# Three token groups' h1 transposed by DMA instead of TensorE, and 28 more blocks of the MLP's first product computed during attention

## The chip, the cores and the metric

One core of a Trainium2 chip runs the whole program. The metric is device time in microseconds (us); lower is better. The engines are TensorE (PE; PEld is its weight loading), VectorE (DVE), ScalarE (ACT), GpSimd (POOL), and SyncE (SP), whose queue issues every DMA of this kernel in program order.

## The reference

All tensors are bf16. S = 2048 tokens, D = 512, F = 1792, 32 heads of 16 columns.

```python
mod = (silu(c) @ w_mod).reshape(1, 6, 1, 512)
sa, ca, ga, sb, cb, gb = mod[:, 0], ..., mod[:, 5]
h = layernorm(x) * (1 + ca) + sa
q, k, v = split_heads(h @ wqkv)                 # 32 heads of 16
p = softmax(where(0 <= i - j < 256, q @ k.T / 4, -1e9))
x = x + ga * (merge_heads(p @ v) @ wo)
h = layernorm(x) * (1 + cb) + sb
h = layernorm(h)                                # the mixer's own norm
u = gelu(einsum('bsd,sf->bdf', h, w1) + b1)     # B1: product over the tokens
y = einsum('bdf,fs->bds', u, w2) + b2           # B2
out = x + gb * y.transpose(0, 2, 1)
```

## The kernel before

**Stages.** A start-up stage loads the inputs, makes the modulation columns `modFM` and the first token group's `h1T`. Attention follows, then a tail with what is left of B1, then B2 with the output.

**Attention.** The 2048 tokens are four groups `tg` of 512 (four row tiles `tl` of 128). In each group the 32 heads are four sets `g8` of 8. Each set has five *units* (k = 0 to 4); so a group is 20 units, numbered `ul` = 5 * g8 + k, and all of attention is 80. A unit is two score tiles `pss` (each two PSUM banks; three buffers), two exponentials `et` on ScalarE (L584), and the products with V into `po`, which has one PSUM bank. After units k = 2 and k = 4 VectorE transposes `po` out of PSUM (`t`, L643); GpSimd divides (`merge`), VectorE transposes back (`OTd`). In group 0 the units k = 0 and k = 3 have half-sized exponentials.

**Dense groups.** The other TensorE work of attention is laid by hand on units in `plan(tg)`: at most one *dense group* a unit. A dense group is 16 column-tiled matmuls (L279, `dense`) into the single PSUM buffer `dn`, which VectorE must empty before the next group may start. There are groups for V (`v_group`), Q and K (`qk_group`), the output projection (`wo_group`, followed by a chain `ln23` of two norms that gives `hb`), and B1 partial sums (`part_group`). In the program, the first exponential of unit u comes first, then the scores of unit u+1, the dense group of unit u, its evacuation, and the products of unit u-1.

**h1T.** For `tg` = 1 to 3, GpSimd applies the first norm (`apply_by_pool`, tile `xn1`, four buffers); TensorE transposes it in two groups of eight 128x128 transposes through `dn` (L261, units 10 and 11 in group 0, 11 and 12 in groups 1 and 2); VectorE evacuates and modulates it in one instruction (L269, `h1T`, one buffer).

**B1 partial sums.** B1 is 14 column blocks `fc` by 16 token blocks `sc`. For the four `fc` in `PART`, `sc` = 0 to 7 are summed in group 3 (32 blocks; two dense groups each, L279 with `hb` and `w1a`) and copied to SBUF (`part`, L742). The tail does the rest: `fc` 0 to 5 for all `sc` (L951), then `fc` 6 to 13 in pairs (L1037), where a partial sum is added back on VectorE (`gelu_a`, L960) before the gelu on ScalarE (L962).

**Order of the engines' work.** It is written out by hand (`manual_schedule`). A planner with estimated clocks (`clock`) decides only where the VectorE chains (norm statistics, norm applications, `norm_rest`, `ln23`) are put between the fixed steps: `fill(until)` places a step if its cost fits. `at_unit` issues the loads: `paced` lets one load follow the first exponential of a unit. On SP's queue the copies of V into `Vc` (L621), the `wmod`, `wod` and `w1a` loads (L793), the `bc` broadcast (L343, L345) and then the `w1b` and `w2r` loads (L933, L935) follow each other in program order. `w1a` holds the first NA token blocks of w1 and is loaded during attention; `w1b` holds the others and is loaded, like `w2r`, into the space that attention frees.

Of the kernel before, what the change touches and what calls it, by code (L numbers as in the profile page):

```python
# [24 lines left out]
NA = 10  # L25
# [5 lines left out]
def kernel(  # L31
# [61 lines left out]
    opool = ctx.enter_context(tc.tile_pool(name="opool", bufs=2))  # L93

    PART = (6, 7, 8, 9)
# [81 lines left out]
    qpool = tc.alloc_tile_pool(name="qpool", bufs=2)  # L177
# [3 lines left out]
    hpool = tc.alloc_tile_pool(name="hpool", bufs=1)  # L181
# [59 lines left out]
    def ln1_apply(tg, tl):  # L241
        xn1[tg, tl] = xp.tile([P, D], DT.bfloat16, name="xn1")
        mean, rstd = ln1[tg][:, tl, 0:1], ln1[tg, tl // 2][:, tl % 2 : tl % 2 + 1]
        if tg:
            apply_by_pool(xn1[tg, tl][:], xres[4 * tg + tl][:], mean, rstd)
        else:
            nc.vector.tensor_scalar(
                out=xn1[tg, tl][:], in0=xres[4 * tg + tl][:], scalar1=mean, scalar2=rstd,
                op0=ALU.subtract, op1=ALU.mult,
            )  # L250


    def transpose_group(tg, pair, pool):
        def mms():
            if pair == 0:
                h1T[tg] = hpool.tile([P, ND, 4 * P], DT.bfloat16, name="h1T")
            pt = pool.tile([P, 2, 4 * P], DT.bfloat16, name="dn")
            for n in range(2):
                dc = 2 * pair + n
                for tl in range(4):  # L260
                    nc.tensor.transpose(  # L261
                        pt[:, n, tl * P : (tl + 1) * P], xn1[tg, tl][:, dc * P : (dc + 1) * P], identity[:]
                    )
            return pt

        def evac(pt):
            for n in range(2):
                dc = 2 * pair + n
                nc.vector.tensor_scalar(  # L269
                    out=h1T[tg][:, dc, :], in0=pt[:, n, :], scalar1=modFM[:, 4 + dc : 5 + dc],  # L270
                    scalar2=modFM[:, dc : dc + 1], op0=ALU.mult, op1=ALU.add,
                )
        return mms, evac, 1.2
# [10 lines left out]
    def v_group(tg, tl, pool, name="dn"):  # L284
        def mms():
            pv = pool.tile([P, D], DT.float32, name=name)
            for dc in range(ND):
                dense(
                    pv, lhsT=h1T[tg][:, dc, tl * P : (tl + 1) * P],
                    rhs=wqkv[:, dc, 2 * D : 3 * D], start=(dc == 0), stop=(dc == ND - 1),  # L290
                )
            return pv

        def evac(pv):
            nc.vector.tensor_copy(out=VaugT[tg][:, tl, :, 0:DH], in_=pv[:].rearrange("p (h d) -> p h d", d=DH))  # L295
            if tl > 1:
                nc.vector.tensor_copy(out=Vc[0][0:64, tl, 0:8, :], in_=VaugT[tg][0:64, tl, 0:8, :])
        return mms, evac, 0.9 if tl > 1 else 0.7

    def qk_group(tg, g8, kind, pool):  # L300
        col0 = g8 * P + (D if kind == "k" else 0)

        def mms():
            pq = pool.tile([P, 4 * P], DT.float32, name="dn")
# [7 lines left out]
        def evac(pq):  # L312
# [5 lines left out]
            QT[tg][g8] = qpool.tile([P, 2, 4 * P], DT.bfloat16, name=f"QT{g8}")  # L318
# [77 lines left out]
    with tc.manual_schedule():  # L396

        with tc.tile_pool(name="modps", bufs=1, space=bass.MemoryType.PSUM) as modps, tc.tile_pool(
# [98 lines left out]
            QT[0][0] = qpool.tile([P, 2, 4 * P], DT.bfloat16, name="QT0")  # L497
# [150 lines left out]
        def norm_rest(tg, g8):  # L648
# [12 lines left out]
            def back():  # L661
                OTd[tg][g8] = opool.tile([P, 4 * P], DT.bfloat16, name=f"OTd{g8}")
                nc.vector.transpose(out=OTd[tg][g8][:], in_=m[:])
# [36 lines left out]
        live = set()  # L700
        loaded = set(range(8))
# [26 lines left out]
        def part_group(fc, k):  # L728
            def mms():
                assert done >= set(range(4 * k, 4 * k + 4))  # L730
                if k == 0:
                    part[fc, "ps"] = ps_dn.tile([P, D], DT.float32, name="dn")
                for sc in range(4 * k, 4 * k + 4):
                    dense(
                        part[fc, "ps"], lhsT=w1box["a"][:, sc, fc * P : (fc + 1) * P], rhs=hb[sc][:],
                        start=(sc == 0), stop=(sc == 7),
# [3 lines left out]
            def evac(ps):  # L740
                if k == 1:
                    nc.vector.tensor_copy(out=part[fc][:], in_=ps[:])  # L742
            return mms, evac, 0.7 * k
# [4 lines left out]
        def plan(tg):  # L748
# [17 lines left out]
            else:  # L766
                for ul, g8, kind in ((2, 1, "k"), (3, 2, "q"), (4, 2, "k"), (5, 3, "q"), (8, 3, "k")):
                    qk(ul, tg, g8, kind)
                for ul in (6, 7, 9, 10):
# [3 lines left out]
            if tg + 1 < NG:  # L773
                t0, t1, q0, v0, k0, q1, v1 = (10, 11, 12, 16, 14, 15, 18) if tg == 0 else (11, 12, 13, 14, 15, 17, 18)
                lay(t0, transpose_group(tg + 1, 0, ps_dn))
                lay(t1, transpose_group(tg + 1, 1, ps_dn))
                lay(v0, v_group(tg + 1, 0, ps_dn))
                lay(v1, v_group(tg + 1, 1, ps_dn))
                for ul, g8, kind in ((q0, 0, "q"), (k0, 0, "k"), (q1, 1, "q")):
                    qk(ul, tg + 1, g8, kind)  # L780
            else:
                for n, fc in enumerate(PART):
                    for k in range(2):
                        lay(12 + 2 * n + k, part_group(fc, k))
# [11 lines left out]
        def at_unit(tg, ul, u, behind):  # L796
            if ul == 0 and tg + 1 < NG:
# [4 lines left out]
                def ap(tl):  # L802
                    ln1_apply(tg + 1, tl)
                    return 1.13
                add_chain((st(1) if tg == 0 else []) + [(lambda tl=tl: ap(tl), 0.0) for tl in range(4)], first=True)
# [62 lines left out]
        for u, (tg, g8, k) in enumerate(units):  # L868
            ul = 5 * g8 + k
            if ul == 0:  # L870
# [149 lines left out]
    with tc.tile_pool(name="gtmp", bufs=2) as gtmp:  # L1020
# [9 lines left out]
        for n, fg in enumerate(fgroups[2:]):  # L1030
            pu = ps_u[n % 2].tile([P, 2, D], DT.float32, name=f"pu{n % 2}")
            for sc in range(NT):
                for i, fc in enumerate(fg):
                    s0 = 8 if fc in PART else 0
# [75 lines left out]
```

## Time and profile before

| What | Value |
|---|---|
| median of 3 runs | 266.26 us (265.99 to 266.61) |
| profiled execution: its own time, and its span in the trace | 268.42 us, 266.7 us |
| mean granted TensorE clock | 0.986 |
| busy share of the span: PE, PEld, DVE, ACT, POOL | 91%, 49%, 63%, 61%, 49% |
| exponentials (L584) | 160, busy 143.6 us |
| start-up, until the first exponential | 17.5 us |
| attention, first to last exponential | 17.5 to 168.9 us |
| rest of B1: L951, then L1037 | to 194.1 us, then to 214.8 us |
| B2 (L1073) | 214.8 to 263.2 us |

How to read it: times are counted from the start of the span. The profiled execution took 1.7 us more than its span, and 2.2 us more than the median of the runs. Shares are averages over stages with different limits: ScalarE is the fullest engine during attention and does little afterwards. In the chain of waits a step is followed back to what released it. In a timeline row the columns are start, duration, engine, line, operation, and the idle time before it with its releaser.

### The profile page before, as it was taken

The numbers are of one execution on the slowest core, as the hardware profiler recorded it, in microseconds if no ns is written. First come the engines' busy times: TensorE is split into PE (matmuls) and PEld (weight loads), VectorE is DVE, ScalarE is ACT, GpSimd is POOL, SyncE is SP. The second block draws the span as 40 slices with busy tenths as digits, with TensorE's granted clock in tenths as the row PEclk, the third lists the DMA queues.
The fourth block names the chain that finished last, engine by engine and source line by source line (L and its number), as shares of the span: only waits on it lengthen the run. The fifth ranks groups of instructions, "written<-read, shape, count | busy, mean of one in ns | idle before, by whom it ended". The sixth has DMA issues, their size and how long they took to land.

```text
span 266.7 us, 11081 instructions
## 1 busy us (share of the span) xinstructions
PE 243.6 (91%) x4933; PEld 129.7 (49%) x4933; DVE 166.9 (63%) x348; ACT 163.7 (61%) x189; POOL 129.4 (49%) x222
## 2 busy tenths in 40 slices
PE   6878988979899889988898999999999999999994
PEld 2434554545555455554555555544444444444443
DVE  6449777886688788798696787689511000523454
ACT  6748887999999999999999999300091110000000
POOL 6102773769476899988997298965200000000000
PEclk9799979999999999999999999999999999999999
DMA  5906984215644534000022000899900000202031
GB/s 173 360 21 160 261 238 153 84 47 144 206 143 112 138 108 117 4 5 5 12 74 72 5 2 5 286 416 420 387 11 0 2 1 0 79 2 79 13 106 39
DMA packets 26084, 29.95 MB, mean 112 GB/s; under 512 B 3252, under 2 KB 23476, under 8 KB 26036
## 3 DMA queue, kind: packets, MB, share of 16 engines
q1 hardware_dynamic: 26036, 29.25, 34.5%
q8 instruction: 38, 0.62, 1.0%
q14 instruction: 10, 0.08, 0.1%
HBM read 22.55 MB, written 2.23 MB: 93 GB/s over the span
## 4 chain that ended last, share of the span: by engine, by line
PE 70%; DVE 18%; ACT 5%; issue 3%; DMA 2%; SPq 1%; ACTq 0%; DVEq 0%
PE py L1073 18%; PE dn L279 18%; PE pu L1037 8%; PE pu L951 7%; PE pss L534 5%; ACT et L584 5%; PE po L595 4%; DVE t L643 3%; PE po L611 3%; DVE qs L317 2%; DVE VaugT L295 2%; DMA wmod<-in_w_mod_dram 2%; PE pss L541 2%; DVE KT L314 2%; DVE x L378 1%
## 5 line engine op out<-in xcount | busy, mean ns | idle before, releaser
L584 ACT ACTIVATE et<-pss 128x1024 bf16<-128x1024 f32 (+1 forms) x160 | 143.6, 992 | 10.0 <-PE pss L541 7.2
L1073 PE MATMUL py<-guT,w2r 128*128 128x512 bf16 (+1 forms) x238 | 48.5, 366 | 0.0
L1052 DVE SCALAR_TENSOR_TENSOR o<-py,bFM,bc 128x512 bf16<-128x512 f32 (+1 forms) x17 | 11.7, 715 | 44.4 <-PE py L1073 44.4
L279 PE MATMUL dn<-h1T,wqkv 128*32 128x512 bf16 x512 | 34.0, 387 | 4.0 <-DVE qs L317 1.5
L534 PE MATMUL pss<-QT,KT 32*128 32x64 bf16 (+2 forms) x704 | 29.6, 237 | 7.6 <-ACT et L584 4.7
L1073 PEld LDWEIGHTS <-w2r 128*128 128x128 bf16 x238 | 23.3, 98 | 25.3
L643 DVE STREAM_TRANSPOSE t<-po 128x512 f32<-128x512 f32 x32 | 22.8, 711 | 12.2 <-PE po L611 11.9
L215 POOL TENSOR_SCALAR ln_ve<-ln_mv 128x1 f32<-128x1 f32 (+1 forms) x40 | 9.5, 237 | 37.2 <-DVE ln_mv L237 20.4
L534 PEld LDWEIGHTS <-KT 32*128 32x128 bf16 x704 | 15.7, 92 | 23.8 <-issue 14.0
L219 POOL TENSOR_TENSOR ln_rstd<-ln_ve,mhalf 128x1 f32<-128x1 f32 (+1 forms) x40 | 23.9, 599 | 3.3
L595 PE MATMUL po<-et,VaugT 128*32 128x64 bf16 (+2 forms) x704 | 25.0, 241 | 0.0
L595 PEld LDWEIGHTS <-VaugT 128*32 128x32 bf16 x704 | 17.2, 96 | 10.8 <-issue 1.7
L279 PEld LDWEIGHTS <-wqkv 128*32 128x32 bf16 x512 | 13.0, 97 | 14.3 <-issue 7.2
L655 POOL TENSOR_TENSOR merge<-t,zr 128x512 bf16<-128x512 f32 x16 | 17.0, 1061 | 5.3 <-DVE zr L654 5.3
L541 PE MATMUL pss<-mask_q,mask_k 32*128 32x256 bf16 (+1 forms) x256 | 19.4, 261 | 0.0
L279 PE MATMUL dn<-wqkv,h1T 128*32 128x512 bf16 x240 | 15.7, 380 | 1.3 <-DVE qs L317 0.8
L962 ACT ACT_TABLE_LOAD x1 | 1.3, 1283 | 24.9 <-PE pu L951 24.9
L687 POOL TENSOR_TENSOR h<-h,bc 128x512 bf16<-128x512 bf16 x12 | 14.0, 1169 | 3.9 <-DVE h L683 3.9
L279 PE MATMUL dn<-wod,OTd 128*32 128x512 bf16 x192 | 12.6, 381 | 2.1 <-DVE KT L314 1.0
L688 POOL TENSOR_TENSOR h<-h,bc 128x512 bf16<-128x512 bf16 x12 | 13.9, 1156 | 0.9
L951 PE MATMUL pu<-hb,w1a 128*128 128x512 bf16 x60 | 13.5, 379 | 0.0
L611 PE MATMUL po<-et,Vc 128*32 128x64 bf16 x960 | 13.0, 194 | 0.0
(110 smaller groups left out, 363.4 us busy)
## 6 DMA issues: line engine op xcount, KB each, us to landing
w2r<-in_B_w_dram SPq DMA_DIRECT2D x14, 512.0 KB, 10.6
w1a<-in_B_w_dram SPq DMA_DIRECT2D x20, 224.0 KB, 2.9
w1b<-in_B_w_dram SPq DMA_DIRECT2D x6, 448.0 KB, 6.3
Vc<-VaugT SPq DMA_DIRECT2D x32, 64.0 KB, 2.5
wmod<-in_w_mod_dram SPq DMA_DIRECT2D x8, 256.0 KB, 4.3
out_dram<-otile SPq DMA_DIRECT2D x15, 128.0 KB, 1.7
x<-in_A_x_dram SPq DMA_DIRECT2D x6, 256.0 KB, 4.5
Vc<-VaugT SPq DMA_DIRECT2D x12, 128.0 KB, 3.6
```

Source lines behind the costliest of these rows:

```text
L219: nc.gpsimd.tensor_tensor(out=r[:], in0=ve[:], in1=mhalf[:, 0:n], op=ALU.pow)
L279: nc.tensor.matmul(out[cols, :], lhsT=lhsT[:, cols], rhs=rhs, start=start, stop=stop, tile_position=(0, 32 * j), skip_group_check=True,)
L534: nc.tensor.matmul(pss[j // 2][:, j % 2, c0 : c0 + nq], lhsT=keys(kb, g8)[rows[j], k0 : k0 + P], rhs=QT[tg][g8][rows[j], par, q0 : q0 + nq ...
L541: nc.tensor.matmul(pss[j // 2][:, j % 2, :].rearrange("p (a r) -> p a r", a=2)[:, 0:n, :] .rearrange("p a (b q) -> p a b q", q=64)[:, :, 0 ...
L584: act = nc.scalar.activation(out=et[:, :, 0:n], in_=state.pop((u, a))[:, :, 0:n], func=ACT.Exp, scale=SCORE_SCALE,)
L595: nc.tensor.matmul(state["po"][32 * j : 32 * j + 32, q0 : q0 + nq], lhsT=VaugT[kb // 4][:, kb % 4, 8 * g8 + 2 * j + par, :], rhs=state["e" ...
L611: nc.tensor.matmul(state["po"][32 * j : 32 * j + 32, q0 : q0 + 64], lhsT=Vc[half][:, b, 8 * g8 + 2 * j + par, :], rhs=state["e", tg, g8, 2 ...
L643: nc.vector.transpose(out=state["t2"][:, par, :], in_=state["po"][:])
L655: nc.gpsimd.tensor_tensor(out=m[:].rearrange("p (b a d) -> p a b d", a=2, d=DH), in0=t2v[:, :, :, 0:DH], in1=zr[:].to_broadcast([P, 2, 16, ...
L951: nc.tensor.matmul(pu[:, i, :], lhsT=w1_of(sc, fc), rhs=hb[sc][:], start=(sc == 0), stop=(sc == NT - 1),)
L1037: nc.tensor.matmul(pu[:, i, :], lhsT=w1_of(sc, fc), rhs=hb[sc][:], start=(sc == s0), stop=(sc == NT - 1),)
L1073: nc.tensor.matmul(pys[n][:, 0 : hi - lo], lhsT=w2r[:, fc, tb * P : (tb + 1) * P], rhs=guT[fc][:, lo:hi], start=(fc == 0), stop=(fc == NF ...
```

## The change

- The transposes of `h1` for groups 1 to 3 leave TensorE. `turn` issues, for each row tile, one DMA transpose of a 128x512 tile from SBUF to SBUF (12 in all, on SP's queue); `modulate` then multiplies and adds in SBUF in place (12 instructions on VectorE, each over one 128x512 slice that needs all four transposes of its group). The planner holds a `modulate` back until four units after the last transpose was issued by its clocks. `h1T` gets two buffers.
- The first norm is applied by VectorE for groups 2 and 3; GpSimd keeps group 1.
- The dense groups are laid anew. Units without one: in group 0 units 9 to 12 and 14 (before 9, 17, 19); in group 1 units 11 and 12 (before 16 and 19); in groups 2 and 3 none (before 16 and 19, and 11).
- `PART` covers fc 6 to 12 for sc 0 to 7 and fc 13 for sc 0 to 3: 60 blocks instead of 32. fc 10, 11 and 12 are summed in two parts, with an added VectorE sum (`part += dn`). The tail's pairs then do 68 matmuls instead of 96.
- NA is 8 instead of 10: `w1a` is 16 loads instead of 20, `w1b` 8 instead of 6.
- The QT tiles share one pool of six buffers; `OTd` 2 and 3 have one buffer each.

```diff
-NA = 10
+NA = 8
...
-    PART = (6, 7, 8, 9)
+    PART = {6: 8, 7: 8, 8: 8, 9: 8, 10: 8, 11: 8, 12: 8, 13: 4}
...
-    hpool = tc.alloc_tile_pool(name="hpool", bufs=1)
+    hpool = tc.alloc_tile_pool(name="hpool", bufs=2)
...
     def ln1_apply(tg, tl):
...
-        if tg:
+        if tg == 1:
             apply_by_pool(xn1[tg, tl][:], xres[4 * tg + tl][:], mean, rstd)
         else:
             nc.vector.tensor_scalar(
...
-    def transpose_group(tg, pair, pool):
...
+    def turn(tg, tl):
+        if tl == 0:
+            h1T[tg] = hpool.tile([P, ND, 4 * P], DT.bfloat16, name="h1T")
+        dma.dma_start_transpose(out=h1T[tg][:, :, tl * P : (tl + 1) * P], in_=xn1[tg, tl][:])
+
+    def modulate(tg, dc):
+        nc.vector.tensor_scalar(
+            out=h1T[tg][:, dc, :], in0=h1T[tg][:, dc, :], scalar1=modFM[:, 4 + dc : 5 + dc],
+            scalar2=modFM[:, dc : dc + 1], op0=ALU.mult, op1=ALU.add,
+        )
...
-        def part_group(fc, k):
+        def part_group(fc, ks, k):
...
             def evac(ps):
-                if k == 1:
+                if k != ks[-1]:
+                    return
+                if ks[0]:
+                    nc.vector.tensor_tensor(out=part[fc][:], in0=ps[:], in1=part[fc][:], op=ALU.add)
+                else:
                     nc.vector.tensor_copy(out=part[fc][:], in_=ps[:])
...
-                for ul, g8, kind in ((2, 1, "k"), (3, 2, "q"), (4, 2, "k"), (5, 3, "q"), (8, 3, "k")):
+                for ul, g8, kind in (
+                    ((2, 1, "k"), (3, 2, "q"), (4, 2, "k"), (5, 3, "q"), (8, 3, "k")),
+                    ((2, 2, "k"), (3, 3, "q"), (4, 3, "k")),
+                    ((2, 3, "q"), (3, 3, "k")),
+                )[tg - 1]:
...
-                for ul in (6, 7, 9, 10):
+                for ul in (6, 7, 9, 10) if tg == 1 else (5, 6, 7, 9):
...
+            for ul, what, n in (
+                ((15, "q", 0), (16, "k", 0), (17, "v", 0), (18, "v", 1), (19, "q", 1)),
+                ((13, "q", 0), (14, "v", 0), (15, "k", 0), (16, "k", 1), (17, "q", 1), (18, "v", 1), (19, "q", 2)),
+                ((12, "q", 0), (13, "v", 0), (14, "k", 0), (15, "k", 1), (16, "q", 1), (17, "v", 1), (18, "q", 2),
+                 (19, "k", 2)),
+                (),
+            )[tg]:
...
+            places, parts = {
+                2: ((8, 10, 11), ((10, (0,)), (11, (0,)), (12, (0,)))),
+                3: (
+                    (4, 8, 10, 11, *range(12, 20)),
+                    ((13, (0,)), (10, (1,)), (11, (1,)), (12, (1,)), *((f, (0, 1)) for f in (6, 7, 8, 9))),
+                ),
+            }.get(tg, ((), ()))
...
                 def ap(tl):
                     ln1_apply(tg + 1, tl)
-                    return 1.13
-                add_chain((st(1) if tg == 0 else []) + [(lambda tl=tl: ap(tl), 0.0) for tl in range(4)], first=True)
+                    turn(tg + 1, tl)
+                    turned[tg + 1] = 20 * tg + now[0] + 4
+                    if tg == 0:
+                        on_pool(1.13)
+                add_chain((st(1) if tg == 0 else []) + [(lambda tl=tl: ap(tl), 0.42 * (tg > 0)) for tl in range(4)]
+                          + [(lambda dc=dc: modulate(tg + 1, dc), 0.42, lambda: 20 * tg + now[0] >= turned[tg + 1])
+                             for dc in range(ND)], first=True)
...
-                    s0 = 8 if fc in PART else 0
+                    s0 = PART.get(fc, 0)
```

## The prediction

> **What bounds the kernel now.** I read the chain of waits first, for the tail, then timelines of ScalarE, TensorE and VectorE, for attention. End of the chain (start, us, what):
>
> ```profile
> 172.99 1.25 PE pa L973 x5
> ...
> 177.26 16.84 PE pu L951 x78
> 194.10 20.72 PE pu L1037 x96
> 214.81 48.40 PE py L1073 x238
> ```
>
> After attention TensorE works without a gap, so a matmul taken out there shortens the run by its own length. ScalarE in attention:
>
> ```profile
> 39.31 2.92 ACT L584 ACTIVATE et<-pss 128x1024 bf16<-128x1024 f32 x4 [0.55 <-PE pss L571]
> 43.58 2.92 ACT L584 ACTIVATE et<-pss 128x1024 bf16<-128x1024 f32 x4 [1.35 <-PE po L611]
> 46.91 1.94 ACT L584 ACTIVATE et<-pss 128x1024 bf16<-128x1024 f32 x2 [0.42 <-PE pss L541]
> ...
> 100.33 35.88 ACT L584 ACTIVATE et<-pss 128x1024 bf16<-128x1024 f32 x38 [0.62 <-PE pss L541]
> 136.37 9.66 ACT L584 ACTIVATE et<-pss 128x1024 bf16<-128x1024 f32 x10 [0.16 <-PE pss L541]
> ```
>
> From group 1 on ScalarE sets the pace: 38 exponentials in 35.88 us, 0.944 each, 1.89 us a unit. Its waits after 39 us in group 0 are 0.55 + 1.35 + 0.42 = 2.3 us, around the two transpose groups. TensorE where each unit already has a dense group (units 13 to 18 of group 3):
>
> ```profile
> 157.43 1.05 PE L279 MATMUL dn<-hb,w1a 128*32 128x512 bf16 x16
> ...
> 163.33 1.05 PE L279 MATMUL dn<-hb,w1a 128*32 128x512 bf16 x16 [0.24 <-DVE part L742]
> ...
> 166.89 1.91 PE L279 MATMUL dn<-hb,w1a 128*32 128x512 bf16 x32
> ```
>
> Five units take 166.89 - 157.43 = 9.46 us, and ten exponentials 9.44: with every unit filled the two engines are level, with nothing to spare.
>
> **The change part by part.**
>
> *B1 out of the tail.* 96 matmuls take 20.72 us, 0.216 each; 28 fewer: **-6.0 us**. The four added `gelu_a` sums and the gelus ride beside them: a pair still takes 16 x 0.216 = 3.45 us, longer than its two sums (2 x 0.69, by L960) or its two gelus (2 x 0.73); the last pair's end about 0.69 + 0.69 + 0.73 = 2.1 us into B2, which needs them only after 48 matmuls, 10 us. Without that cover they would cost 2.1. Two more `w1b` loads (448 KB each, 0.92 MB at about 410 GB/s, 2.2 us): `w2r`'s last issue is at 185.1 and lands 8 to 11 us later, so near 198 after; B2 then starts near 209. Zero.
>
> *Entering the tail.* One statistics step (0.64 + 0.18 us) instead of two lies ahead of the last `OTd`; GpSimd's `merge` (1.06) then limits: **-0.4**.
>
> *Dense work in attention.* Seven more dense groups, +7 x 1.05 = 7.4 us of TensorE; six transpose groups go, of 0.61 to 1.03 each, about -4.4. ScalarE hides it while it is the slower: groups 2 and 3 now have 40 filled units, 8 stretches of five. At 9.46 against 9.44 this is +0.2; if the 0.24 us wait for `dn` falls due on half of the units, +4.8. VectorE decides which. In group 2 it was busy 32.6 of 38.7 us; it gains four norm applications and four modulations (8 x 0.54, by L683's mean), three `part` copies and one more evacuation (4 x 0.68) and loses four L269 (0.535 each): 4.3 + 2.7 - 2.1 = +4.9, less what of the `ln23` chains slips into group 3, so about 90% instead of 84%. As 38 exponentials ran without a wait at 84%, I take **+1.0**. GpSimd loses 8 x (0.27 + 0.77) = 8.3 us; it ends nothing there.
>
> *Thin stretches.* Group 1 now has two empty units running, group 0 four. The trace shows a price for that (busy us of PE, PEld, DVE, ACT, POOL, then granted clock, DMA share, GB/s):
>
> ```profile
> 34.00:37.00 3.00, 1.85 (x49) 1.09 (x49) 2.41 (x7) 2.93 (x5) 2.79 (x6) 1.00 0.73 198
> 37.00:41.00 4.00, 4.00 (x104) 2.56 (x92) 2.54 (x6) 3.45 (x4) 2.43 (x4) 0.57 0.89 283
> ```
>
> Three us with TensorE busy 62% were followed by about 3.5 us at half clock. Units 11 and 12 of group 1 will be as thin for 4.6 us, just ahead of filled ones; 3.5 us at half clock lose 1.75 us of TensorE work. Between 0 and 1.75 I take **+0.8**. (The Trainium skill, "TensorE: Matmul & The Clock Gate", section "What's actually happening", says that the clock halves after an idle window of about 3.4 us. Read strictly, 62% busy is no idle window and this term would be 0, the total 0.8 lower; the rows above speak for the harsher reading.)
>
> *The DMA transposes.* The trace has none. The nearest rows are the copies between SBUF tiles, in the table of DMA issues (KB each, us to landing) and in SP's timeline:
>
> ```profile
> Vc<-VaugT SPq DMA_DIRECT2D x32, 64.0 KB, 2.5
> Vc<-VaugT SPq DMA_DIRECT2D x12, 128.0 KB, 3.6
> ```
>
> ```profile
> 30.90 1.25 SPq L621 DMA_DIRECT2D Vc<-VaugT  x2
> 32.83 1.25 SPq L621 DMA_DIRECT2D Vc<-VaugT  x2
> 34.18 3.24 SPq L793 DMA_DIRECT2D wmod<-in_w_mod_dram  x5
> ```
>
> An SBUF-to-SBUF copy of 128 KB lands after 3.6 us, and copies follow each other after 0.63. So four transposes are done between 3 x 0.63 + 2.5 = 4.4 us after the first issue (overlapping) and 4 x 3.6 = 14.4 (one by one); a gain is excluded, since nothing used these DMAs before. I take the lower end with 3.6 to land, as the copies overlap. A `modulate` waits in VectorE's order, and evacuations queue behind it. In group 1, by the order of the changed program, the fourth transpose is issued near 61.2 and `modulate` follows unit 5's Q copy at 67.3; in group 2, 100.1 and 106.1. Six us cover 3.6: no cost. Group 0 is tighter. GpSimd starts the four applications at 30.60 and needs 1.1 us each, so the fourth transpose is issued near 35.0, but `modulate` stands right behind this row:
>
> ```profile
> 34.74 0.15 DVE L357 CAST bFM<-dn 128x30 f32<-128x30 bf16 x1
> ```
>
> It stalls from 34.9 to 38.6, and the next `po` evacuation (37.41 before), with three modulations and an `OTd` ahead of it, comes near 40.9. ScalarE has then up to three score buffers in hand, 2.8 us, so some 0.7 of the 3.5 shows. On SP's queue the transposes stand ahead of two `Vc` copies and the five `wmod` loads: the last of these is issued near 39.4 instead of 36.8, lands 4.3 later near 43.7, and the `bc` product wants it near 41.5 (43.3 before, less the transposes). TensorE waits 2, of which some 1 reaches ScalarE. Against this stand the 2.3 us of waits around the removed transposes. Group 0 between -2.3 and +4: I take **-0.5**.
>
> Sum: -6.0 - 0.4 + 1.0 + 0.8 - 0.5 = **-5.1 us**. On the profiled execution's 268.42 us that is 263.3; on the median of the runs, which lies 2.16 below, 266.26 - 5.1 = **261.1 us**.
>
> **The rivals.**
>
> *Slow transposes (slower).* One mechanism: the four transposes of a group run one by one, t us each, and `modulate` stalls VectorE, with `dn` and `po` unemptied behind it. With the first issue at 31.7, 58.7 and 97.3, `modulate` at 34.9, 67.3 and 106.1, and 2.8 us of scores in hand, groups 0, 1 and 2 lose 4t - 6.0, 4t - 11.4 and 4t - 11.6. At t = 2.8 the first loss (5.2) eats the whole gain; at 3.6, the landing of a like copy, the loss is 8.4 + 3.0 + 2.8 = 14.2 and the time 275. For it: no row shows a transpose, and each element of a row goes to another partition. Against it: copies of the same size overlap. Chance 0.30. (The Trainium skill, "VectorE: DVE Perf Modes", section "The three transpose paths", gives 1309 ns for a 128x128 block by DMA; if the four blocks of a tile add up, an estimate from it is t = 5.2 and a time of 295. No run here shows it.)
>
> *VectorE or `dn` binds in the filled groups.* The +4.8 end: 265. Against it: the 38 exponentials without a wait at 84%. Chance 0.13.
>
> *Attention gains too.* Group 0 gets its whole 2.3, no thin stretch costs anything, filled units run level: -6.0 - 0.4 - 2.3 + 0.2 = -8.5, or 257.8. Chance 0.11.
>
> **How the numbers follow.** The forecast, 259 to 264, has 0.46. Faster by over 0.2% (0.5 us, about what a measurement of this kernel can tell from none): all of the forecast, 0.11, 0.09 of the second rival, 0.02 of the first (t under 2.7): 0.68. Within 0.2%: 0.02 + 0.02. Slower: 0.26 of the first and 0.02 of the second. The range reaches from the third rival to t = 3.3 of the first: 257.5 to 272.
>
> **What would show it.** Right: L1037's successor takes 68 matmuls and 14.7 us; attention ends within 2 us of its old end; transposes land within 4 us; no VectorE idle ahead of `modulate` outside group 0. Wrong: idle time ahead of `modulate` released by a DMA in groups 1 and 2; `dn` waits on most units of groups 2 and 3; a clock under 1 after unit 12 of group 1 for more than 3.5 us.

## The result, and the profile after

The changed kernel takes **272.92 us** (median of 4 runs, 272.71 to 274.01) against 266.12 beside it: ratio **1.025, 95% interval 1.0202 to 1.0298**, so it is slower by 5.4 to 7.9 us. Ratios here and below leave disturbed runs out, so they can differ a little from the ratio of two medians; of e2 that leaves two runs of four, and e2's profile is of a disturbed one. The forecast was 261.1, faster.

The profiled execution has a span of 272.3 us (266.7 before) and a mean TensorE clock of 0.962 (0.986). I divide both spans at the same events: a group of attention is 40 exponentials and reaches from the start of its first to the start of the next group's first.

| stretch, us | before | after | difference |
|---|---|---|---|
| start to first exponential | 17.5 | 15.5 | -2.0 |
| group 0 | 36.2 | 43.8 | +7.7 |
| group 1 | 38.2 | 42.8 | +4.6 |
| group 2 | 38.7 | 39.2 | +0.6 |
| group 3 | 38.4 | 39.0 | +0.6 |
| last exponential to B2 | 45.9 | 40.0 | -5.9 |
| B2 to the end | 51.9 | 51.9 | 0.0 |

The first row differs between executions of one kernel too (15.4 to 17.9 over the profiles of this study), so it is no effect of the change. The other rows are the change's: the tail gave what was promised, and two groups of attention lost twice as much (12.3 against 5.9 us). Differences are taken before rounding.

The end of the chain of waits (start, us, what) answers to the lines of L951, L1037 and L1073 before. The product that took 96 matmuls and 20.72 us now takes 68 and 14.63:

```profile
205.71 8.42 PE pu L1058 x39
214.18 6.21 PE pu L1058 x28
220.38 4.53 PE py L1094 x21
```

ScalarE in attention (start, us; the bracket is the idle time before, and who ended it). Groups 2 and 3 look as before, batches of 18 and 20 exponentials without a wait. Groups 0 and 1 do not:

```profile
42.81 1.08 ACT L579 ACTIVATE et<-pss 128x512 bf16<-128x512 f32 x2 [4.22 <-PE pss L536]
48.61 1.08 ACT L579 ACTIVATE et<-pss 128x512 bf16<-128x512 f32 x2 [2.20 <-PE pss L536]
53.70 2.92 ACT L579 ACTIVATE et<-pss 128x1024 bf16<-128x1024 f32 x4 [1.78 <-PE pss L566]
71.00 4.82 ACT L579 ACTIVATE et<-pss 128x1024 bf16<-128x1024 f32 x5 [4.00 <-PE pss L536]
...
110.83 17.21 ACT L579 ACTIVATE et<-pss 128x1024 bf16<-128x1024 f32 x18 [0.93 <-PE pss L536]
128.21 18.96 ACT L579 ACTIVATE et<-pss 128x1024 bf16<-128x1024 f32 x20 [0.17 <-PE pss L536]
```

**Group 0** is read on three queues. SP's queue (how long each issue held it), then VectorE, then TensorE:

```profile
31.03 7.18 SPq L258 DMA_TRANSPOSE h1T<-xn  x4
38.26 1.27 SPq L616 DMA_DIRECT2D Vc<-VaugT  x2
39.63 2.60 SPq L808 DMA_DIRECT2D wmod<-in_w_mod_dram  x5
```

```profile
32.73 0.15 DVE L352 CAST bFM<-dn 128x30 f32<-128x30 bf16 x1
39.55 0.41 DVE L261 TENSOR_SCALAR h1T<-h1T,modFM 128x512 bf16<-128x512 bf16 x1 [6.66 <-DMA h1T<-xn]
```

```profile
41.88 0.40 PE L590 MATMUL po<-et,VaugT 128*32 128x256 bf16 x4 [5.35 <-DVE t L638]
45.65 1.04 PE L328 MATMUL dn<-wmod,sT_rep 128*32 128x512 bf16 x8 [0.50 <-DMA wmod<-in_w_mod_dram]
```

The four transposes hold SP's queue for 7.18 us. VectorE stands 6.66 us behind its first modulation, with the evacuation of `po` queued behind; TensorE waits 5.35 us for that evacuation and ScalarE 4.22 for TensorE's scores. Then the product for `bc` still waits for `wmod`, 0.9 us in all. The issue of `wmod`'s last load ends at 42.2, which is 26.8 us after the first exponential; before it was 37.4, or 19.9 us after.

The queue had no room for them. Some lines of SP's timeline of the kernel before:

```profile
23.58 3.35 SPq L793 DMA_DIRECT2D x<-in_A_x_dram  x2
...
27.61 2.08 SPq L621 DMA_DIRECT2D Vc<-VaugT  x2
...
37.52 0.93 SPq L793 DMA_DIRECT2D wod<-in_A_wo_dram  x2
```

From 19.20 to 38.45 its rows add up to 18.3 of 19.25 us: what is put into a full queue delays everything behind it by nearly its whole length, here by 26.8 - 19.9 = 6.9 of 7.18 us.

TensorE's clock in the same stretch (us; busy us of PE, PEld, DVE, ACT, POOL; granted clock, DMA share, GB/s):

```profile
32.00:35.00 3.00, 1.79 (x49) 1.01 (x49) 0.79 (x2) 2.92 (x5) 2.90 (x5) 1.00 0.96 171
35.00:38.00 3.00, 1.51 (x76) 0.91 (x65) 0.00 (x0) 3.00 (x4) 1.31 (x3) 0.82 0.71 50
38.00:41.00 3.00, 0.00 (x0) 0.00 (x0) 1.46 (x4) 0.59 (x1) 0.00 (x0) 0.50 0.50 117
...
54.00:57.00 3.00, 2.58 (x64) 1.34 (x59) 1.73 (x4) 2.62 (x4) 0.87 (x2) 1.00 0.00 0
```

The half clock begins at 36.9 us: a mean of 0.82 from 35 to 38 is 1.1 us at 0.50. That is only 0.4 us after TensorE's last matmul (36.5), and in the 3.4 us before it TensorE was busy for 2.49. So the long wait did not bring the drop about. The kernel before has one at nearly the same place (37.3 us, after 2.26 busy of 3.4), and so has e1 below, which does not have the waits; there it lasts 3.4 us. Here, with the waits behind it, it lasts 17 us, until 54.0.

**Group 1** is another story. VectorE's norms for group 2, and GpSimd's foldings of `wod` beside them, from the two timelines:

```profile
63.66 3.51 DVE L249 TENSOR_SCALAR xn<-x,ln_mv,ln_rstd 128x512 bf16<-128x512 bf16 x3
...
68.19 0.40 DVE L249 TENSOR_SCALAR xn<-x,ln_mv,ln_rstd 128x512 bf16<-128x512 bf16 x1
```

```profile
64.68 3.51 POOL L804 TENSOR_TENSOR wod<-wod,bc 128x512 bf16<-128x512 bf16 x3
```

Three norms take 1.17 us each while GpSimd's operations of 1.17 run; the fourth, alone, takes 0.40. The copy of V behind the three comes late, TensorE waits 2.85 us for it, and ScalarE the 4.00 us at 71.00.

### The profile page after: what moved, and what is told of

Same layout as the page of the kernel before. It is cut to its first block, busy times and chain, and to the rows that moved or that the text cites. A ratio compares the mean times of both kernels' runs of the same rounds, so it can differ in the third digit from the quotient of the medians.

```text
span 272.3 us, 11163 instructions
## 1 busy us (share of the span) xinstructions
PE 240.4 (88%) x4960; PEld 128.6 (47%) x4969; DVE 178.0 (65%) x367; ACT 164.7 (60%) x189; POOL 121.7 (45%) x206
## 3 DMA queue, kind: packets, MB, share of 16 engines
HBM read 22.55 MB, written 2.23 MB: 91 GB/s over the span
## 4 chain that ended last, share of the span: by engine, by line
PE 63%; DVE 22%; DMA 4%; POOL 4%; SPq 3%; issue 2%; ACT 1%; DVEq 0%; ACTq 0%; POOLq 0%
PE dn L272 20%; PE py L1094 18%; PE pu L972 8%; PE pu L1058 5%; DMA wmod<-in_w_mod_dram 4%; DVE VaugT L289 3%; PE pss L529 3%; DVE t L638 3%; DVE KT L309 3%; PE po L590 3%; PE po L606 2%; DVE qs L312 2%; DVE xn L249 2%; DVE ln_stats L666 2%; PE pa L994 1%
## 5 line engine op out<-in xcount | busy, mean ns | idle before, releaser
L272 PE MATMUL dn<-h1T,wqkv 128*32 128x512 bf16 x512 | 35.1, 397 | 8.0 <-DVE VaugT L289 5.8
L529 PE MATMUL pss<-QT,KT 32*128 32x192 bf16 (+2 forms) x704 | 27.9, 243 | 4.8 <-ACT et L579 2.3
L1073 DVE SCALAR_TENSOR_TENSOR o<-py,bFM,bc 128x512 bf16<-128x512 f32 (+1 forms) x17 | 11.7, 716 | 30.5 <-PE py L1094 30.5
L590 PE MATMUL po<-et,VaugT 128*32 128x64 bf16 (+2 forms) x704 | 25.8, 247 | 5.4 <-DVE t L638 5.4
L590 PEld LDWEIGHTS <-VaugT 128*32 128x32 bf16 x704 | 18.6, 98 | 17.0 <-issue 7.5
L529 PEld LDWEIGHTS <-KT 32*128 32x128 bf16 x704 | 14.7, 93 | 20.1 <-issue 11.7
L272 PE MATMUL dn<-hb,w1a 128*32 128x512 bf16 x240 | 15.5, 380 | 1.7 <-DVE part L743 1.2
L272 PE MATMUL dn<-wod,OTd 128*32 128x512 bf16 x192 | 12.6, 381 | 2.9 <-DVE x L373 1.3
L682 POOL TENSOR_TENSOR h<-h,bc 128x512 bf16<-128x512 bf16 x12 | 13.9, 1155 | 2.0 <-DVE h L678 2.0
L981 DVE TENSOR_TENSOR gelu_a<-pu,part 128x512 f32<-128x512 f32 x8 | 5.2, 686 | 14.6 <-PE pu L1058 14.6
L316 POOL TENSOR_SCALAR QT<-qs,mask_even 128x512 bf16<-128x512 bf16 x14 | 9.8, 703 | 10.8 <-DVE qs L312 10.8
```

The costliest lines, as they stand in the source:

```text
L272: nc.tensor.matmul(out[cols, :], lhsT=lhsT[:, cols], rhs=rhs, start=start, stop=stop, tile_position=(0, 32 * j), skip_group_check=True,)
L529: nc.tensor.matmul(pss[j // 2][:, j % 2, c0 : c0 + nq], lhsT=keys(kb, g8)[rows[j], k0 : k0 + P], rhs=QT[tg][g8][rows[j], par, q0 : q0 + nq ...
L590: nc.tensor.matmul(state["po"][32 * j : 32 * j + 32, q0 : q0 + nq], lhsT=VaugT[kb // 4][:, kb % 4, 8 * g8 + 2 * j + par, :], rhs=state["e" ...
L682: nc.gpsimd.tensor_tensor(out=h2[:], in0=h2[:], in1=bc_cb1, op=ALU.mult)
```

## The experiments

Two theories for the loss. **Queue theory:** the transposes lengthen SP's full queue, so that `wmod` and the modulations are late (group 0), and the foldings collide with VectorE's new norms (group 1). **Rivals:** that the place of the modulations alone is at fault, that TensorE's half clock in the emptied units is the cause, or that transposes of this kind are slow wherever they stand. Each edit is one of the changed kernel, unless it names another. "Against before" is the ratio less one, times 266.3 us.

| run | edit | median | ratio (95%) | against before, us |
|---|---|---|---|---|
| after | | 272.9 | 1.0250 (1.0202 to 1.0298) | +6.7 |
| e1 | group 1's h1 on TensorE | 263.7 | 0.9902 (0.9865 to 0.9939) | -2.6 |
| e2 | foldings later | 272.4 | 1.0130 (1.0051 to 1.0209) | +3.5 |
| e3 | e1 and e2 | 264.0 | 0.9890 (0.9825 to 0.9955) | -2.9 |
| e4 | modulations later | 273.7 | 1.0266 (1.0202 to 1.0329) | +7.1 |
| e5 | transposes behind `wmod` | 268.6 | 1.0041 (0.9995 to 1.0087) | +1.1 |
| e6 | `wmod` loaded earlier | 271.6 | 1.0149 (1.0090 to 1.0209) | +4.0 |
| e7 | e1 without the 28 blocks | 268.5 | 1.0047 (1.0003 to 1.0092) | +1.3 |
| e8 | matmuls in the empty units | 273.4 | 1.0213 (1.0145 to 1.0280) | +5.7 |
| e9 | e5 and e2 | 266.5 | 0.9965 (0.9916 to 1.0014) | -0.9 |
| e10 | e9, earlier loads and transposes | 271.6 | 1.0179 (1.0102 to 1.0255) | +4.8 |
| e11 | e1, foldings earlier | 263.8 | 0.9909 (0.9870 to 0.9948) | -2.4 |
| e12 | e11, group 2's norm on GpSimd | 266.6 | 1.0021 (0.9976 to 1.0065) | +0.6 |

**e1: group 1's h1 back on TensorE.** Groups 2 and 3 keep their DMA transposes, and all 60 B1 blocks stay.

```diff
+                lay(10, transpose_group(1, 0, ps_dn))
+                lay(11, transpose_group(1, 1, ps_dn))
...
                     ln1_apply(tg + 1, tl)
+                    if tg == 0:
+                        on_pool(1.13)
+                        return
                     turn(tg + 1, tl)
                     turned[tg + 1] = 20 * tg + now[0] + 4
-                    if tg == 0:
-                        on_pool(1.13)
...
```

> Group 1's h1 goes back to TensorE (two transpose groups on units 10 and 11 of group 0, evacuated and modulated by VectorE); groups 2 and 3 keep the DMA transposes, everything else stays as changed. Theory A (in group 0 the four DMA transposes follow each other by 1.2 us and more on SP's queue, VectorE stalls 6.7 us on the first modulate, po stays full, the clock halves, and the wmod loads behind the transposes make the bc product wait): ScalarE's waits of 4.2, 2.2 and 1.8 us between 40 and 54 us shrink to about the 2.3 us of the kernel before; the time falls by some 6 us, to about 267. Rival (the new places alone, with four thin units in a row, let the clock halve and cost the same): the clock still halves after unit 9 and the time stays above 271.

By the ratios it is 9.3 us faster than the changed kernel, and faster than the kernel before by 1.6 to 3.6 us. ScalarE's waits in 37 to 50 are 1.03 us or less, and the two groups of eight transposes took 1.03 and 0.99 us of TensorE:

```profile
37.50 2.92 ACT L603 ACTIVATE et<-pss 128x1024 bf16<-128x1024 f32 x4 [0.77 <-PE pss L590]
40.80 7.92 ACT L603 ACTIVATE et<-pss 128x1024 bf16<-128x1024 f32 x10 [0.38 <-PE pss L560]
...
60.75 7.69 ACT L603 ACTIVATE et<-pss 128x1024 bf16<-128x1024 f32 x8 [1.56 <-PE pss L560]
```

Group 0 takes 36.1 us (43.8 changed, 36.2 before) and group 1 40.3 (42.8 changed). So the four transposes of one group cost more than all that the change had to gain. In group 1 one folding is done before the norms, since `bc` is there earlier; two still lie beside them, and three norms take 2.72 us.

**e2: the foldings of `wod` later,** in units 3 and 4 of group 1.

```diff
-                then[18] = [(lambda g=g: fold_wod(g), 0.0) for g in range(ND)]
...
+            if tg == 1 and ul in (3, 4):
+                for g in (2 * ul - 6, 2 * ul - 5):
+                    fold_wod(g)
+                    on_pool(1.16)
```

> The only edit to the changed kernel: GpSimd's four foldings of ga into wod (1.16 us each) move from the start of group 1 to after its unit 3. Theory B (VectorE's three norm applications at 63.7 us took 1.17 us each because each waited for a GpSimd instruction on SBUF, and the V evacuation behind them came 2.9 us late): the three applications take 0.4 to 0.6 us each, the 2.85 us wait of dn and the 4.0 us wait of ScalarE behind it shrink to under 1; time about 269. Rival (the applications are slow for another reason, such as the DMA transposes that read xn at that time): they stay above 1 us and the time stays at 273.

VectorE's norms and modulations, then ScalarE:

```profile
65.93 1.05 DVE L249 TENSOR_SCALAR xn<-x,ln_mv,ln_rstd 128x512 bf16<-128x512 bf16 x3
67.75 0.40 DVE L249 TENSOR_SCALAR xn<-x,ln_mv,ln_rstd 128x512 bf16<-128x512 bf16 x1
75.28 3.21 DVE L261 TENSOR_SCALAR h1T<-h1T,modFM 128x512 bf16<-128x512 bf16 x3
```

```profile
69.43 7.62 ACT L579 ACTIVATE et<-pss 128x1024 bf16<-128x1024 f32 x8 [0.31 <-PE pss L536]
78.48 1.94 ACT L579 ACTIVATE et<-pss 128x1024 bf16<-128x1024 f32 x2 [1.43 <-PE pss L536]
```

Without the foldings beside them, three norms take 1.05 us, not 3.51, and the wait of 4.00 is 0.31. The foldings now lie beside the modulations, which become 1.07 each, with a wait of 1.43. Group 1 is 2.1 us shorter (42.8 to 40.7), group 0 nearly as long as without the edit (43.5). The profile of e9, which has the same edit, shows the same: three norms in 1.04 us, and waits of 0.31 and 1.43. The collision is shown; the edit moves part of it.

**e3: both edits.** The diff is that of e1 and that of e2.

> Edits of both: group 1's h1 by TensorE, and the foldings after unit 3 of group 1. Theories A and B together: the two gains add up, 6 + 4: about 263, faster than the kernel before by about 3, since the tail's 6 us remain and the filled units of groups 2 and 3 cost about 2. Rival (filled units without a spare on TensorE eat the tail's gain by themselves): 266 or more.

No gain over e1 (-2.9 against -2.6, intervals overlap; group 1 40.2 against 40.3): the gains of e1 and e2 were expected to add up, and do not. With TensorE's transposes the collision costs less.

**e4: group 1's modulations held back eight units, not four.**

```diff
-                    turned[tg + 1] = 20 * tg + now[0] + 4
+                    turned[tg + 1] = 20 * tg + now[0] + (4 if tg else 8)
```

> The only edit to the changed kernel: the planner holds group 1's modulations back 8 units instead of 4, which puts them behind unit 11 and the bc evacuation, after the transposes have landed (39.5 us). Theory A says that the stall is a matter of place: VectorE no longer waits for a DMA, ScalarE's 4.2 us wait goes, the wmod loads are as late as before, so that the bc product still waits; time 269 to 270. Rival (the transposes' load on SP's queue, not VectorE's order, is what costs): the wmod loads hold the bc product until 48 us in any case, and the time stays above 271.5.

VectorE's wait of 6.66 is 0.39, and the time is not better, because the product for `bc` waits in its place. TensorE, then ScalarE:

```profile
43.60 0.59 PE L328 MATMUL dn<-wmod,sT_rep 128*32 128x512 bf16 x1 [2.82 <-DMA wmod<-in_w_mod_dram]
46.38 1.87 PE L328 MATMUL dn<-wmod,sT_rep 128*32 128x512 bf16 x13 [2.20 <-DMA wmod<-in_w_mod_dram]
```

```profile
48.78 1.08 ACT L579 ACTIVATE et<-pss 128x512 bf16<-128x512 f32 x2 [6.73 <-PE pss L536]
```

Of two waits in series, the later one sets the time. That the modulations stand too early is not the cause by itself.

**e5: the transposes behind `wmod` on SP's queue,** with the modulations from unit 14.

```diff
                     ln1_apply(tg + 1, tl)
+                    if tg == 0:
+                        on_pool(1.13)
+                        return
                     turn(tg + 1, tl)
...
+            if tg == 0 and ul == 9:
+                for tl in range(4):
+                    turn(1, tl)
+                turned[1] = 14
```

> The changed kernel with one thing moved: the four DMA transposes of group 1's rows are issued after unit 9 of group 0, behind the last load of wmod on SP's queue, and its modulations are held until unit 14. Queue theory (the transposes take 5.8 to 7.2 us of issue on SP's queue, and all that is behind them is late by that): wmod is there in time again (last issue about 36, before the product for bc), VectorE does not wait, the 4.22 and 2.20 us waits of ScalarE in 42 to 50 go, and group 0 is 5 to 6 us shorter, less what the loads of wod (now behind the transposes) and the modulations (fourth transpose issued about 42, landing about 45) still cost the first q of group 1 at unit 15, up to 2 us: 267 to 269, with the collision of group 1 left as it was. Rival (the transposes are slow wherever they stand, so that group 1's first product waits for them): the same 4 us of wait moves to units 15 and 16, and the time stays at 271 to 273.

SP's queue, then VectorE:

```profile
32.24 3.26 SPq L808 DMA_DIRECT2D wmod<-in_w_mod_dram  x5
35.72 6.14 SPq L258 DMA_TRANSPOSE h1T<-xn  x4
```

```profile
45.21 1.38 DVE L261 TENSOR_SCALAR h1T<-h1T,modFM 128x512 bf16<-128x512 bf16 x4 [2.60 <-DMA h1T<-xn]
```

The edit brings 5.6 us (+6.7 to +1.1): group 0 takes 37.6 instead of 43.8. It changes the order of the queue and the place of the modulations; since e4 moved the modulations alone and gained nothing, the order is what was missing. The remaining wait for the fourth transpose is 2.60 on VectorE and 2.37 on ScalarE. The rival of 271 to 273 is out. While the transposes run, the DMA share rises above 1 (transfers overlap in it) and little is moved (last two columns: DMA share, GB/s):

```profile
35.00:38.00 3.00, 2.29 (x88) 1.37 (x87) 2.90 (x8) 2.93 (x5) 2.67 (x6) 1.00 0.95 308
38.00:41.00 3.00, 2.30 (x68) 1.21 (x69) 2.49 (x6) 2.63 (x4) 1.85 (x5) 1.00 1.58 120
```

**e6: `wmod` loaded two a unit, in units 2 to 5,** with e4's edit.

```diff
-            if tg == 0 and 2 <= ul < 10:
-                v, js = (2, 4, 3, 5)[ul // 2 - 1], slice(ul % 2 * 2, ul % 2 * 2 + 2)
+            if tg == 0 and 2 <= ul < 6:
+                for i in (2 * ul - 2, 2 * ul - 1):
+                    v, js = (2, 4, 3, 5)[i // 2 - 1], slice(i % 2 * 2, i % 2 * 2 + 2)
```

> The changed kernel with wmod's eight loads issued two a unit in units 2 to 5 of group 0 (not one a unit in 2 to 9), so that all stand ahead of the transposes on SP's queue, and group 1's modulations held back eight units instead of four. Queue theory: neither VectorE's wait of 6.7 us nor the product's wait for wmod is left, group 0 is 5 to 7 us shorter than in the changed kernel (about 37 to 38 us for its 40 exponentials): 266 to 268, with group 1's collision left. Rival (holding back the modulations or the product alone is no help because TensorE's half clock is what costs): ScalarE still waits 4 us or more in 40 to 50 and the time stays above 271. If the earlier loads hold up the rows of x that group 2 and 3 need, VectorE's statistics wait for a DMA in units 2 to 8.

A miss of mine, but not of the theory: the last two loads still stood behind the transposes, as SP's queue shows, and the product waited 2.96 us for them, ScalarE 4.31 behind it. By the ratios the edit gains 2.7 us, half of e5's. But ScalarE's wait of over 4 us and a time above 271 are also what the rival, the half clock, asked for, so this run does not part the two.

```profile
33.10 6.18 SPq L258 DMA_TRANSPOSE h1T<-xn  x4
39.33 1.27 SPq L616 DMA_DIRECT2D Vc<-VaugT  x2
40.71 1.97 SPq L808 DMA_DIRECT2D wmod<-in_w_mod_dram  x2
```

**e7: e1 with 32 B1 blocks in attention, as before the change.**

```diff
-    PART = {6: 8, 7: 8, 8: 8, 9: 8, 10: 8, 11: 8, 12: 8, 13: 4}
+    PART = {6: 8, 7: 8, 8: 8, 9: 8}
...
+                3: (tuple(range(12, 20)), tuple((f, (0, 1)) for f in (6, 7, 8, 9))),
```

> The fastest kernel so far (group 1's transposes on TensorE, groups 2 and 3 by DMA; 263.7) with the 28 added B1 blocks taken back to the tail: only the 32 of before are computed in attention. By the sum of the prediction the tail is 6.0 us longer; attention gets back what the 28 blocks cost in groups 2 and 3: nothing if those units were bound by ScalarE (269 to 270), 2 us by the two groups' +1 each seen in the trace (267 to 268), and 6 if the blocks only moved work (263 to 264).

3.9 us slower than e1 by the ratios (1.0047 - 0.9902); between the two profiled executions it is 5.9. There the tail is 5.6 us longer and attention the same (154.5 against 154.2): group 3 is 1.2 us shorter, but group 2, with units 8, 10 and 11 now empty, 1.7 longer. One window of it shows TensorE at half clock behind the empty units:

```profile
117.00:120.00 3.00, 3.00 (x50) 1.38 (x44) 2.13 (x5) 2.38 (x3) 2.65 (x8) 0.52 0.03 5
```

So the 28 blocks cost attention nothing in sum. Of group 2's 1.7 us a ScalarE wait of 0.91 at 120.3 follows the half clock; another of 1.13 at 100.6 lies at full clock and is not explained.

**e8: 16 dense matmuls in each of the units 9 to 12 and 14 of group 0,** into an accumulator that nothing reads.

```diff
+                for ul in (9, 10, 11, 12, 14):
+                    lay(ul, warm_group(ps_dn))
```

> The changed kernel with 16 dense matmuls into an unused accumulator added in each of the units 9 to 12 and 14 of group 0 (the places that the transposes and the products of group 1 have left empty); nothing reads them. Waiting theory (SP's queue and VectorE's wait hold the product for bc and the copies; the half clock only follows from that): ScalarE's wait of about 4 us in 42 to 47 stays, and the time is within 2 us of the changed kernel's 272.9: 271 to 274. Clock theory (TensorE has too little to do, is given half its clock from 36 to 54, and that is what the seven us are): the clock stays near 1.0 up to 48, group 0 is 4 to 6 us shorter, 267 to 269.

TensorE, then ScalarE:

```profile
36.75 1.05 PE L272 MATMUL dn<-h1T,wqkv 128*32 128x512 bf16 x16
40.66 0.40 PE L600 MATMUL po<-et,VaugT 128*32 128x256 bf16 x4 [2.87 <-DVE t L648]
```

```profile
41.60 1.08 ACT L589 ACTIVATE et<-pss 128x512 bf16<-128x512 f32 x2 [2.90 <-PE pss L546]
44.76 1.94 ACT L589 ACTIVATE et<-pss 128x1024 bf16<-128x1024 f32 x2 [2.08 <-PE po L616]
```

Filling the units kept the granted clock at 1.00 up to 40 us, and at 0.61 to 0.82 from there to 52 (the changed kernel: 0.50 from 39 to 54). TensorE still waits 2.87 us for the evacuation, ScalarE 2.90 and 2.08. Group 0 takes 44.0 us (43.8 without the edit), and ScalarE's waits in it add up to the same 12.6 us. So filling the emptied units takes nothing off: VectorE still waits for the transposes until 38.9 us (39.6 without), and the product for `wmod` until 46.7. What the half clock costs by itself stays open. In group 0 it still held for 6.8 us (17.1 without the edit), and the added matmuls take at least 5 x 1.05 us of TensorE themselves.

**e9: e5 and e2 together,** that is, the change with its two collisions mended. The diff is that of e5 and that of e2.

> The changed kernel with both places mended and all three DMA transpositions kept: group 1's four transposes behind wmod's last load with the modulations at unit 14 (which alone gave 268.6), and GpSimd's four foldings of wod behind unit 3 of group 1 instead of at the end of group 0 (which alone took ScalarE's 4 us wait at group 1's start to 0.3 and gave a new one of 1.4). If these two collisions are all that was lost: 268.6 less 2 to 4, so 265 to 266.5, of which 2 us are still the first modulation's wait for the fourth transpose at 45. If the gains do not add (as with TensorE's transposes and the moved foldings, 264.0 against 263.7): 268 to 269.

Group 0 takes 37.1 and group 1 41.6 us; the two gains add within the noise (5.6, and 2.0 more by the ratios; e2 alone had brought 3.2), and the result is level with the kernel before.

**e10: the same with `wmod` two a unit and the transposes after unit 6, modulations from unit 13.**

```diff
+            if tg == 0 and ul == 6:
+                for tl in range(4):
+                    turn(1, tl)
+                turned[1] = 13
```

> As the kernel before it, but wmod's eight loads are issued two a unit in units 2 to 5 and the four transposes behind them, after unit 6, with the modulations from unit 13: the transposes are issued about 33 to 39 and have landed by 43, before the modulations' place, and wmod is there before its product. Queue theory: no wait of VectorE for a DMA, group 0 as short as before the change (36 to 37.5 us for its 40 exponentials), and the whole 262 to 264.5, level with the kernel whose group 1 is transposed on TensorE (263.7) or under it by the 1.7 us that TensorE's two groups of transposes no longer take. Rival (a transpose of this kind slows what moves beside it, loads of wmod and rows of x among them, wherever it stands): a wait of 2 us or more for a DMA shows in group 0 all the same, and the time is 266 or more.

I had the transposes issued from about 33 to 39. With all loads drawn ahead, they came at 38.66 (this execution began its exponentials 2.4 us later than e9's), and VectorE's wait was back. SP, then VectorE:

```profile
38.66 5.83 SPq L258 DMA_TRANSPOSE h1T<-xn  x4
```

```profile
46.75 0.73 DVE L261 TENSOR_SCALAR h1T<-h1T,modFM 128x512 bf16<-128x512 bf16 x2 [5.34 <-DMA h1T<-xn]
```

Moving work within a full queue does not make room: counted from the first exponential, the fourth transpose landed at 28.8 us, and in e9 at 28.9, while the modulations stand a unit earlier here. The last transpose landed some 2.2 us after its issue had ended (44.5), so most of the time goes into the queue ahead of the transposes and into their issue. A wait over 2 us is there and the time is above 266, as the rival had it; the rows of SP's queue account for it, and this run does not show that the transposes slow what moves beside them.

**e11: e1 with the foldings after units 16 and 17 of group 0.**

```diff
+            if tg == 0 and ul in (16, 17):
+                for g in (2 * ul - 32, 2 * ul - 31):
+                    fold_wod(g)
+                    on_pool(1.16)
```

> The fastest kernel so far (group 1's h1 transposed on TensorE, groups 2 and 3 by DMA: 263.7) with GpSimd's four foldings of wod issued after units 16 and 17 of group 0, as soon as bc has landed (49.8 there), instead of from unit 18 on, where three of them lie beside VectorE's norms and modulations in group 1. Contention theory: VectorE's operations from SBUF to SBUF in bf16 (norm, modulation) take 0.40 instead of up to 1.2 us, group 1's 40 exponentials take 38 instead of 40.5 us, and the time is 261 to 262.5. Rival (the 2.8 us that group 1 is over the kernel before are its denser units, not the foldings): group 1 stays at 40 or more and the time at 263.5 to 264; moving the foldings to units 3 and 4 of group 1 had given 264.0.

All norms take 0.35 to 0.40 us, as the contention theory had it, but the time is the rival's, that of e1 (0.9909 against 0.9902). Group 1 has 39.7 us, 0.6 less, and group 2 has 1.0 more. So the collision is worth little once group 1's transposes are on TensorE. That group 1 stays 1.5 us above the 38.2 of before is left open.

**e12: e11 with group 2's norm on GpSimd.**

```diff
-        if tg == 1:
+        if tg in (1, 2):
             apply_by_pool(xn1[tg, tl][:], xres[4 * tg + tl][:], mean, rstd)
```

> As the kernel before it, with group 2's norm applied by GpSimd (as before the change) and not by VectorE: what the change of engine for that norm is worth once nothing collides with it. VectorE is freed of four operations of 0.40 us at the start of group 1, GpSimd gets 4 x 1.04 us. If VectorE's share is what stretches group 1, 0.5 to 1.5 us less than the kernel before; if not, no difference (within 0.5).

Neither of the two: about 3 us slower (1.0021 against 0.9909). GpSimd has its four norms done at 61.5, not VectorE's 57.7, the transposes follow, and group 1 gets group 0's wait. SP, VectorE and ScalarE:

```profile
58.22 6.31 SPq L258 DMA_TRANSPOSE h1T<-xn  x4
```

```profile
67.66 0.73 DVE L261 TENSOR_SCALAR h1T<-h1T,modFM 128x512 bf16<-128x512 bf16 x2 [3.81 <-DMA h1T<-xn]
```

```profile
72.00 1.94 ACT L603 ACTIVATE et<-pss 128x1024 bf16<-128x1024 f32 x2 [4.50 <-PE pss L560]
```

So from the last norm to the first modulation a group needs 67.7 - 61.5 = 6 us, also where no loads of `wmod` are about. VectorE's earlier norms kept group 1 clear of this.

**Where the 6.7 us come from,** by the ratios: e7, which is the change without group 1's transposes and without the 28 blocks, is +1.3; the 28 blocks bring -3.9 (e7 to e1); group 1's DMA transposes cost +9.3 (e1 to the changed kernel), of which 5.6 are their place on SP's queue, 2.0 the foldings, and 1.7 are left when both are mended (e9 to e1). By the intervals of the ratios each of these differences is known to about 1.7 us, so the last two are barely clear of nothing. e1, e3 and e11 are faster than both kernels, by about 1% against the kernel before.

## Why the prediction was wrong, point by point

- **B1 out of the tail (-6.0): right.** Measured -6.1 (20.72 to 14.63). B2 came 5.9 earlier against the last exponential, so the entry of the tail gave nothing, where -0.4 was forecast.
- **Filled units of groups 2 and 3 (+1.0 for both): right.** 1.2 in the profile, 0.6 in each. The rival in which `dn` or VectorE binds there is out.
- **Thin stretches (+0.8 in group 1): not met in the changed kernel, but the mechanism is there.** The clock stayed at 1.00 through the thin units of group 1 (75 to 93 us). In e5, e9 and e10, which leave the same units empty, it was 0.50 for 3.4 us from 85.4, 81.1 and 88.3 us, in or just behind unit 13, after 3.4 us in which TensorE was busy for 1.98, 2.23 and 2.23. Their plan for group 1 is the changed kernel's, so as far as these runs show it was spared by chance. What such a drop costs was not separated. On the four empty units of group 0 the forecast put no price; there the half clock lasted 17 us, with the waits. The page "TensorE: Matmul & The Clock Gate" of the Trainium skill, in "What's actually happening", lets the clock halve after an idle window of about 3.4 us. These drops do not agree with that, nor does the changed kernel's at 36.9 us (2.49 of 3.4 us busy) or e7's at 117.1 (2.59); its drop at 67.6, behind TensorE's wait of 2.85 us, comes nearest (0.74).
- **The DMA transposes in group 0 (-0.5, between -2.3 and +4): the step that failed.** Group 0 measured +7.7, and with its transposes back on TensorE (e1) nothing. Three parts of the step were off.
  First, the issue: 0.63 us each was taken from the copies' rows, and in group 0 a transpose held SP's queue for 1.4 to 1.8 us on average (5.5 to 7.2 for four, over the runs that have them there). `wmod`'s last issue was forecast 2.6 us later than before and came 6.9 later, counted from the first exponential.
  Second, VectorE's stall, counted from the first exponential of each profile, began where it was forecast (17.4 us) but ended at 24.1, not 21.1: 6.7 us, not 3.7.
  Third, the price at ScalarE: "some 0.7 of the 3.5" and "some 1" of TensorE's 2 took both waits as mostly covered by scores in hand. They came one behind the other, with TensorE at half clock throughout, and ScalarE waited 7.6 us more than before in this group (12.6 against 5.0). How much of that is the half clock was not separated. The order of the queue was in the forecast; that it had no room was not: its rows in the profile of before show 95% of the stretch taken.
- **Groups 1 and 2, transposes at no cost: right in the changed kernel** (no modulation there waits for a DMA), and e12 shows the cover was real and thin: four us less of it cost 4.5 us of wait.
- **Norms on VectorE at 0.54 each: wrong for the first three.** 1.17 beside GpSimd, 0.40 alone. This is the part of group 1's +4.6 that could be explained: e2 took 2.1 off. The other 2.5 are open. The profile of before already had the same sign, a copy of V between SBUF tiles (L297) that took 0.64 us beside GpSimd's `merge` and 0.22 two us later; the forecast did not count with it. The Trainium skill, "SBUF — State Buffer", section "SBUF: two separate sides", says that VectorE in a two-port mode and GpSimd take a shared pair of ports for the whole instruction, and the other blocks; the trace agrees, with norms lasting as long as GpSimd's instructions, 1.17 us. The ports themselves no run here shows.
- **The rival of slow transposes:** right in direction and in the engine that stalls, wrong in mechanism. The transposes do not run one by one at 3.6 us or more; they are issued 1.4 to 1.8 us apart in group 0 and land, in the changed kernel, 2.3 to 4.4 us after issue. At 1.8 its formula for group 0 (4t - 6.0) gives 1.2 us, and nothing in groups 1 and 2. The estimate of t = 5.2 from the Trainium skill, "VectorE: DVE Perf Modes", section "The three transpose paths", does not hold for these tiles.

Part of the six us that four transposes last is the issue itself: group 2's in the changed kernel (from 64.95 us) held the queue 1.20 to 1.26 us each, at a DMA share of 0.32. What stretches single ones to 2.8 us, SP's queue or the fullness of the 16 DMA engines (a share of 1.58 at 120 GB/s in e5), was not separated. Nor did any run put the transposes on a queue other than SP's, which would be the direct test.

## What to carry to other kernels

A transfer that replaces TensorE work is paid on the queue it is put into: add up that queue's rows in the stretch, and if they fill it, count the new instructions' whole length against everything behind them. Two waits of different engines in one stretch must both be mended before either shows a gain. And when an operation moves to VectorE, look at what GpSimd does at that time, since a 0.40 us operation can take 1.17 beside it.

## What the runs showed of the hardware

- A DMA transpose of a 128x512 bf16 tile from SBUF to SBUF holds SP's queue for 1.2 us at the median and for up to 2.8, where a copy of V holds it for 0.6 at the median; four follow in 5.2 to 7.3 us, and one lands 2.3 to 5.5 us after its issue began (all profiles).
- While four of them ran in e5, the DMA share rose from 0.95 to 1.58 and the rate fell from 308 to 120 GB/s.
- A drop to half clock does not need an idle TensorE, and its busy time alone does not decide: 2.49 of 3.4 us busy was followed by a drop in the changed kernel (36.9 us), and 1.71 of 3.4 us by none in e1 (55.4 to 58.8 us).
- The half clock outlasted the wait by far: TensorE had work again at 41.9, and was given 0.50 up to 54, through windows in which it was busy 2.1 to 3.0 of 3 us. Why so long was not tried.
